# Block products for the streamed second matmul of the first MLP, in a linear-attention and two-MLP kernel

## The chip, the cores and the metric

One core of a Trainium2 chip (trn2). The metric is device time in microseconds, the median of several executions. In the profile PE is TensorE, DVE VectorE, ACT ScalarE; SP is the sync engine, whose queue issues nearly every DMA here.

## The reference

Batch 4, 8 heads, 768 steps, head size 64; 3072 tokens of 512 features go through two MLPs of width 2048.

```python
state = gamma * state + k_t v_t^T ;  y_t = q_t state / 8      # linear attention, per head
x = y laid out as (3072 tokens, 512)
h = x @ w_in ;  g = h * sigmoid(1.702 h) ;  x = g @ w_out     # first MLP,  512 -> 2048 -> 512
h = x @ w_in2 ; g = max(h,0) + alpha * min(h,0) ; out = g @ w_out2   # second MLP, same shape
```

The weights arrive as float64 words, so the kernel converts them to float32 itself. Every float32 product is made of float32r matmuls over a high and a low part: hi·hi, lo·hi and hi·lo.

## The kernel before

Activations are kept transposed, in blocks of 512 tokens. A matmul is 128x128 by 128x512.

**Stages.** Attention runs in 24 chunks of 128 steps. Token blocks 0 and 1 of the first MLP are computed from resident weights while these are converted (`mlp_h`, `mlp_y`); then comes the streamed part. It works on five pairs of two token blocks each, `PAIRS`: pairs 0 and 1 are blocks 2 to 5 of the first MLP, pairs 2 to 4 are the six blocks of the second.

**Units.** In the streamed part `x @ w_in` is done as seven block products instead of eight (Strassen's scheme in Winograd's form). For one pair and one slice pair of the width (2 x 128 features, eight of them: the code calls it a quad) there are seven units; each is six matmuls on one loaded weight tile `hw` (`h_unit`, line 617). The weight sums that the scheme needs are made once (`conv_sums`, `conv_split`) and stored to DRAM in `wc`; the input sums are made by `x_prep` just before a pair begins. The outputs of the units are added on DVE (line 632) and copied on ACT (line 629) out of two PSUM banks of each of two pools. There are 280 units in 40 groups of seven; below, group 0 is the first, and groups 0 to 15 belong to pairs 0 and 1. The attention chunks 16 to 23 still run among groups 0 to 4.

**Chunks.** `g @ w_out` follows 32 units later (`YLAG`) in chunks of six matmuls, one after each unit. For pairs 2 to 4 it is done in seven block products too: `strassen_y`, line 711, weights `yw`, over two halves of four slice pairs, with sums of g made by `y_split` on DVE (line 660), splits into high and low (`g_split`: ACT line 492, DVE line 493) and sums of the results by `y_out` on DVE (line 722). For pairs 0 and 1 it is plain: 768 matmuls at line 526, weights `woh` and `wol` from `wo`, which holds the converted `w_out` as it is, in a ring of six (`WSTEPS`, `load_wo`); eight chunks follow seven units.

**Order and queues.** The Tile scheduler fixes at build time the order of instructions on every engine, from the program's order and priorities; each engine then runs its queue in that order. `jobs` is a table of slots (two slots for each group of seven units, `base` = 64 being the first) in which conversions (`convert`), stores, sums, loads of x and attention steps are put. SBUF tiles come from a ring of 82 slots of 2 KB per partition (`take`, `give`); raw inputs go through five buffers `ld` of twice that. All loads and stores share SP's queue.

Of the kernel before, what the change touches and what calls it, by code (L numbers as in the profile page):

```python
# [31 lines left out]
WSTEPS = 6  # L32
# [26 lines left out]
IDX_S = 2  # L59
ATT1 = 36  # L60
W2_AT = [7 + m // 2 for m in range(10)] + [16 + m - 10 for m in range(10, 22)] + [32 + 4 * (m - 22) // 5 for m in range(22, 32)]
# [3 lines left out]
def tile_linear_attention_two_mlps(ctx: ExitStack, tc, qk, kv, w1, w2, consts, alpha, out):  # L65
# [34 lines left out]
        for k, l in (("in", 1), ("in", 2), ("out", 2))  # L100
        for i in range(NQ)
    }
    wo = {f: dram.tile([2, P, 512], F32, name=f"wo{f}", tag=f"wo{f}") for f in range(NF)}
# [32 lines left out]
    def issue(limit=RING):  # L136
        while count["issued"] < min(len(order), count["done"] + limit):
            key = order[count["issued"]]
            if key[0] == "x" and ("x", key[1]) not in stored:
                return  # L140
# [73 lines left out]
    def conv_lo(key):  # L214
# [10 lines left out]
        if kind == "in" or layer == 2:  # L225
            raw[key] = t
        else:
            give(t)
# [10 lines left out]
    def store(key):  # L239
        kind, layer, ft = key  # L240
        hi, lo = w_hi[key], w_lo.get(key)
        if kind == "out" and layer == 1:
            put(wo[ft][0], hi)
            put(wo[ft][1], lo)
        else:
            dst, at = wc[kind, layer, ft // 2], W_AT[kind]
            if packed(key) is not None:
                put(dst[at["a22" if kind == "in" else "a11"]], hi)
            elif kind == "out" or ft % 2 == 0:
                first = at["a11" if kind == "in" else "a12"]  # L250
                put_two(dst, first, 0, hi)
                put_two(dst, first, 1, lo)
            else:
                put(dst[at["a22"], :, 0:256], hi[:, 256:])
                put(dst[at["a22"], :, 256:512], lo[:, 256:])
# [6 lines left out]
    def conv_sums(kind, layer, i):  # L262
        a, b = raw.pop((kind, layer, 2 * i)), raw.pop((kind, layer, 2 * i + 1))
# [10 lines left out]
        give(a, b)  # L274
# [120 lines left out]
    def att_x(c):  # L395
# [23 lines left out]
        if c % (2 * BT // C) == 2 * BT // C - 1:  # L419
            stored.add(("x", idx))  # L420
            issue()
# [24 lines left out]

    def x_prep(idx, n):
        which = X_OF[n]
        for k in range(2):
            b11, b12 = halves2(loaded["x", idx, k, 0])  # L450
            b21, b22 = halves2(loaded["x", idx, k, 1])
            sub = lambda o, x, y: nc.vector.tensor_tensor(out=o, in0=x, in1=y, op=ALU.subtract)
            if which == "t2":
                t1, t2 = xt[idx, "t1", k], xt[idx, "t2", k] = take("t1"), take("t2")
                sub(t1, b12, b11)
                sub(t2, b22, t1)
            if which == "t3":
                xt[idx, "t3", k] = take("t3")
                sub(xt[idx, "t3", k], b22, b12)
            if which == "t4":  # L460
                xt[idx, "t4", k] = t = xt.pop((idx, "t2", k))
                sub(t, b21, t)
            if which[0] == "b":
                x_split(idx, n, k, {"b11": b11, "b21": b21, "b22": b22}[which])
# [4 lines left out]
            if which in ("b22", "t4"):  # L469
                done()  # L470
# [105 lines left out]
    def load_y(c):  # L576
        if c < len(ychunks) and ychunks[c][0] == "s":
            _, idx, grp, p, m = ychunks[c]
            load_piece(yw, "yw", "out", PAIRS[idx][0], GQ * grp + m, p)

    ysteps = [(idx, t, f if t == 0 else NF - 1 - f) for idx in range(IDX_S) for t in range(2) for f in range(NF)]
    wkey = [f for _, _, f in ysteps]
    wring = {}
    ychunks = [("o", n, half) for n in range(len(ysteps)) for half in range(2)]
    ychunks += [
        ("s", idx, grp, p, m)
        for idx in range(IDX_S, len(PAIRS))
# [4 lines left out]

    def load_wo(n):
        for f in wkey[n:n + 2 * WSTEPS]:
            if f in wring:
                continue
            if len(wring) == WSTEPS or ("out", 1, f) not in stored:
                return
            wring[f] = take("woh", dtype=F32R), take("wol", dtype=F32R)
            for t, src in zip(wring[f], (0, 1)):  # L600
                nc.sync.dma_start(out=t.bitcast(F32), in_=wo[f][src])
# [45 lines left out]
    def y_split(c):  # L647
        kind = ychunks[c][0]
        with tc.high_priority(HG):
            if kind == "o":  # L650
                _, n, half = ychunks[c]
                if half == 0:
                    idx, t, f = ysteps[n]
# [327 lines left out]
```

## Time and profile before

| | |
|---|---|
| median of 3 runs | 1070.77 us (1069.96 to 1071.54) |
| the profiled execution | 1073.08 us, of which the span is 1071.3 us |
| PE busy | 1052.1 us, 98% of the span |
| DVE busy | 774.2 us, 72% |
| ACT busy | 628.2 us, 59% |
| DMA | 283.5 MB, 265 GB/s in the mean |

Busy time counts an engine's instructions from their start to their end, and these overlap in a full queue, so the distance between two starts is shorter than the mean of one. The DMA share is the mean busy share of the 16 DMA engines.

### The profile page before, as it was taken

Reading aid. Unit: us, or ns where it says so; the run is one execution under the profiler, and the core shown is the slowest. Engines: PE = TensorE matmul, PEld = TensorE weight load, DVE = VectorE, ACT = ScalarE, POOL = GpSimd, SP = SyncE. Lnnn points to the kernel's source line nnn. Section 1 sums busy time; section 2 is a strip of 40 time slices with the busy share of each in tenths; the row PEclk is TensorE's granted clock in tenths of the full one; section 3 lists DMA queues with packets and bytes.
Section 4 is the critical chain, followed back from the end, with each engine's and each line's share of the span. In section 5 each row is a group of like instructions: output and inputs, shape, how many; then the busy total and the mean of one; then the engine's idle time right before and its main releaser. Section 6 shows DMA issues by size and latency. Waiting matters only on the chain.

```text
span 1071.3 us, 16434 instructions
## 1 busy us (share of the span) xinstructions
PE 1052.1 (98%) x5644; PEld 861.1 (80%) x5644; DVE 774.2 (72%) x1370; ACT 628.2 (59%) x1220; POOL 0.2 (0%) x4
## 2 busy tenths in 40 slices
PE   8999999999979999999999999999999999999998
PEld 5788877788758888888888888888888888888887
DVE  6999835455469786556577889699677698677693
ACT  6787724344466475455475766585555675546750
POOL 0000000000000000000000000000000000000000
PEclk9999999999999999999999999999999999999999
DMA  7688659988989997988969998866776566776561
GB/s 288 218 277 314 204 173 343 372 301 290 318 284 314 374 356 253 390 300 275 392 216 325 316 323 292 278 199 228 231 256 186 177 218 201 221 238 198 174 207 70
DMA packets 163156, 283.53 MB, mean 265 GB/s; under 512 B 15744, under 2 KB 63232, under 8 KB 163072
## 3 DMA queue, kind: packets, MB, share of 16 engines
q1 hardware_dynamic: 162784, 282.27, 78.4%
q8 instruction: 45, 0.74, 0.3%
q14 instruction: 39, 0.32, 0.1%
q10 hardware_dynamic: 288, 0.20, 0.1%
HBM read 212.15 MB, written 70.25 MB: 264 GB/s over the span
## 4 chain that ended last, share of the span: by engine, by line
PE 88%; DMA 7%; ACT 2%; DVE 2%; SPq 0%; issue 0%; DVEq 0%; ACTq 0%
PE py L526 24%; PE py L711 21%; PE pa L617 18%; PE pd L617 14%; PE ph L505 7%; DMA ld<-kv 3%; DMA hw<-wcin 1%; PE sc L317 1%; ACT v L310 1%; DMA xsd<-x 1%; PE px L353 1%; DMA ld<-w 1%; PE pu L353 1%; DMA early<-qk 1%; PE px L365 0%; DMA wcin<-slo 0%
## 5 line engine op out<-in xcount | busy, mean ns | idle before, releaser
L617 PE MATMUL pa<-xo,hw 128*128 128x512 f32 x960 | 244.6, 392 | 7.5 <-ACT gw L629 5.6
L617 PEld LDWEIGHTS pa<-xo,hw 128*128 128x128 f32 x960 | 180.4, 189 | 46.7 <-ACT gw L629 6.1
L493 DVE TENSOR_TENSOR gl<-gw,gh 128x512 fp32r<-128x512 f32 x208 | 140.0, 685 | 63.4 <-ACT gh L492 48.6
L617 PE MATMUL pd<-xo,hw 128*128 128x512 f32 x720 | 184.1, 392 | 0.0
L711 PE MATMUL py<-gh,yw 128*128 128x512 f32 x672 | 179.8, 389 | 0.0
L492 ACT CAST gh<-gw 128x512 fp32r<-128x512 f32 x208 | 126.6, 620 | 73.0 <-PE py L711 15.2
L617 PEld LDWEIGHTS pd<-xo,hw 128*128 128x128 f32 x720 | 135.7, 189 | 28.6
L711 PEld LDWEIGHTS py<-gh,yw 128*128 128x128 f32 x672 | 126.2, 188 | 26.1
L711 PE MATMUL py<-gl,yw 128*128 128x512 f32 x336 | 103.6, 389 | 0.0
L526 PE MATMUL py<-gh,woh 128*128 128x512 f32 x256 | 99.6, 389 | 0.0
L526 PE MATMUL py<-gh,wol 128*128 128x512 f32 x256 | 99.6, 389 | 0.0
L483 ACT ACTIVATE t<-gw 128x512 f32<-128x512 f32 x72 | 45.5, 632 | 73.6 <-DVE gw L632 73.0
L485 DVE SCALAR_TENSOR_TENSOR gw<-t,nalpha,gw 128x512 f32<-128x512 f32 x96 | 71.3, 746 | 23.7 <-ACT gw L484 23.1
L526 PE MATMUL py<-gl,woh 128*128 128x512 f32 x256 | 79.3, 389 | 0.0
L711 PEld LDWEIGHTS py<-gl,yw 128*128 128x128 f32 x336 | 63.1, 188 | 13.1
L629 ACT COPY gw<-pa 128x512 f32<-128x512 f32 x80 | 46.6, 583 | 37.0 <-PE pa L617 36.8
L310 ACT ACTIVATE v<-ld,cst 128x64 f32<-128x64 f32 x168 | 43.9, 336 | 40.5 <-DMA ld<-kv 39.8
L632 DVE TENSOR_TENSOR gw<-pd,gw 128x512 f32<-128x512 f32 x80 | 54.7, 685 | 16.2 <-PE pd L617 15.3
L526 PEld LDWEIGHTS py<-gh,wol 128*128 128x128 f32 x256 | 48.1, 188 | 10.0
L526 PEld LDWEIGHTS py<-gh,woh 128*128 128x128 f32 x256 | 48.1, 188 | 10.0
L526 PEld LDWEIGHTS py<-gl,woh 128*128 128x128 f32 x256 | 48.1, 188 | 9.9
L722 DVE TENSOR_TENSOR yc<-py,yc 128x512 f32<-128x512 f32 x59 | 37.9, 682 | 20.5 <-PE py L711 20.5
(94 smaller groups left out, 1572.1 us busy)
## 6 DMA issues: line engine op xcount, KB each, us to landing
hw<-wcin SPq DMA_DIRECT2D x280, 256.0 KB, 4.5
yw<-wcout SPq DMA_DIRECT2D x168, 256.0 KB, 3.1
ld<-w SPq DMA_DIRECT2D x64, 512.0 KB, 5.1
woh<-wo SPq DMA_DIRECT2D x46, 256.0 KB, 5.4
wol<-wo SPq DMA_DIRECT2D x46, 256.0 KB, 5.5
ld<-qk SPq DMA_DIRECT2D x21, 512.0 KB, 5.3
ld<-kv SPq DMA_DIRECT2D x21, 512.0 KB, 5.2
ld<-xsd SPq DMA_DIRECT2D x20, 512.0 KB, 6.0
```

The lines of the kernel that those rows point to most:

```text
L310: nc.scalar.activation(out=v[:, h, :], in_=vt[:, h * D:(h + 1) * D], func=AF.Copy, scale=decay_v[:, h:h + 1])
L483: nc.scalar.activation(out=t, in_=src, func=AF.Relu, scale=-1.0)
L485: nc.vector.scalar_tensor_tensor(out=g, in0=t, scalar=nalpha[:, ft:ft + 1], in1=g, op0=ALU.mult, op1=ALU.add)
L492: nc.scalar.copy(out=gh, in_=g)
L493: nc.vector.tensor_tensor(out=gl, in0=g, in1=gh.bitcast(F32), op=ALU.subtract)
L505: nc.tensor.matmul(out=ph, lhsT=w[:, k * P:(k + 1) * P], rhs=x[:, k, :], start=(n == 0), stop=(n == len(prods) - 1),)
L526: nc.tensor.matmul(out=py[e], lhsT=w, rhs=g, start=(begin and seen[e] == 1), stop=(end and seen[e] == 3))
L617: nc.tensor.matmul(out=ps, lhsT=w[:, 256 * part_ + k * P:256 * part_ + (k + 1) * P], rhs=x[2 * k + low], start=(n in (0, 1, 3) and m == 0) ...
L629: nc.scalar.copy(out=chain[quad, n], in_=ps)
L632: nc.vector.tensor_tensor(out=g, in0=ps, in1=g, op=ALU.add)
L711: nc.tensor.matmul(out=ps[e], lhsT=w[:, at:at + P], rhs=t, start=(fresh and seen[e] == 1), stop=(m == GQ - 1 and seen[e] == 3), skip_group ...
L722: add_ = lambda o, x: nc.vector.tensor_tensor(out=o, in0=ps, in1=x, op=ALU.add)
```

## The change

Pairs 0 and 1 get their `g @ w_out` as block products too: all 280 chunks are now of one kind, one after each unit. For this the first MLP's `w_out` gets sums and an arranged copy in `wc`, as the other three weights have; its float32 words are stored to `wraw` and loaded again later for the sums. The tiles `woh` and `wol`, `wo` and `load_wo` go. The loads of x take eight slot tiles `xl` instead of four `ld` buffers, and are put two slots later for pairs 1 to 4. The second MLP's weight conversions (`W2_AT`), the stores of the first's weights (`STORE_W`) and the sums of `w_in` and `w_out` (`SUMS_IN`, `SUMS_OUT`) get other slots.

```diff
+YLOAD = 28
+SUMS_IN = 37
+SUMS_OUT = [58, 60, 62, 65, 72, 74, 76, 78]
+STORE_W = (28, 1.2)
-W2_AT = [7 + m // 2 for m in range(10)] + [16 + m - 10 for m in range(10, 22)] + [32 + 4 * (m - 22) // 5 for m in range(22, 32)]
+W2_AT = [1 + 2 * m for m in range(5)] + [10 + 1.07 * (m - 5) for m in range(5, 32)]
...
-            give(t)
+            put(wraw[ft // 2][:, ft % 2, :], t)
+            give_stored(t)
...
-        a, b = raw.pop((kind, layer, 2 * i)), raw.pop((kind, layer, 2 * i + 1))
+        if ("raw", i) in loaded and (kind, layer) == ("out", 1):
+            a, b = halves2(loaded.pop(("raw", i)))
+        else:
+            a, b = raw.pop((kind, layer, 2 * i)), raw.pop((kind, layer, 2 * i + 1))
...
+    def x_load(idx):
+        assert ("x", idx) in stored
+        for k in range(2):
+            for d in range(2):
+                for t in range(2):
+                    xl[k, d, t] = take("xl")
+                    nc.sync.dma_start(out=xl[k, d, t], in_=xsd[idx][k, :, d, t])
...
     def y_chunk(c):
-        if ychunks[c][0] == "o":
-            _, n, half = ychunks[c]
-            idx, t, f = ysteps[n]
-            first, end = n % NF == 0, n % NF == NF - 1
-            mlp_y(1, 2 * PAIRS[idx][1] + t, f, first, end, None, wring[f], range(2 * half, 2 * half + 2))
...
-    def strassen_y(c):
-        _, idx, grp, p, m = ychunks[c]
+        idx, grp, p, m = ychunks[c]
...
-            s = slot + 3 if key[1] == 2 else ATT1 + 1 + 4 * i if i < 4 else base + 2 * i - 6
+            s = slot + 3 if key[1] == 2 else SUMS_IN + 3 * i if key[0] == "in" else SUMS_OUT[i]
...
-            y_turn(min(8 * past // NU, old) + max(0, past - old * NU // 8))
+            y_turn(past)
```

How instructions stand now is read from the built programs. The first place is DVE's queue about the end of pair 0: from the add of unit 54 (pair 0's last add) to the first add of pair 1, that of unit 57. Before, the first add is row 527 and the second row 541; the last twelve rows are these (`gl` is a low part of g, `xo` an input of pair 1's units, `cvt` a weight in conversion, `slo` a low part of a weight sum).

```order
530 L445 TENSOR_TENSOR xo<-ld,xo 128x512
531 L493 TENSOR_TENSOR gl<-gw,gh 128x512
532 L445 TENSOR_TENSOR xo<-ld,xo 128x512
533 L281 TENSOR_TENSOR slo<-s_4404,shi 128x512
534 L183 TENSOR_SCALAR cvt<-cvt 128x512
535 L186 TENSOR_SCALAR cvt<-cvt 128x512
536 L493 TENSOR_TENSOR gl<-gw,gh 128x512
537 L445 TENSOR_TENSOR xo<-t_4333,xo 128x512
538 L493 TENSOR_TENSOR gl<-gw,gh 128x512
539 L445 TENSOR_TENSOR xo<-t_4343,xo 128x512
540 L189 ISA cvt<-cvt,cvr 128x1024
541 L632 TENSOR_TENSOR gw<-pd,gw 128x512
```

In the changed kernel the two adds are rows 588 and 612 of DVE's queue; the last twelve rows are these (`t` is an input sum of pair 1, `xl` its loaded x).

```order
601 L452 TENSOR_TENSOR xo<-xl,xo 128x512
602 L452 TENSOR_TENSOR xo<-t_4626,xo 128x512
603 L467 TENSOR_TENSOR t_4513<-xl,t_4513 128x512
604 L467 TENSOR_TENSOR t_4523<-xl,t_4523 128x512
605 L511 TENSOR_TENSOR gl<-gw,gh 128x512
606 L274 TENSOR_TENSOR s_4703<-cvt 128x256
607 L274 TENSOR_TENSOR s_4703<-cvt,s_4702 128x256
608 L226 TENSOR_TENSOR wlo<-cvt,whi 128x512
609 L452 TENSOR_TENSOR xo<-t_4513,xo 128x512
610 L452 TENSOR_TENSOR xo<-t_4523,xo 128x512
611 L511 TENSOR_TENSOR gl<-gw,gh 128x512
612 L636 TENSOR_TENSOR gw<-pd,gw 128x512
```

Between the two adds stood 13 instructions, and now 24: row 593, not shown, counts two. The inputs of pair 1 were mostly made earlier, and stand here now.

The second place is SP's queue at the same point. Before, these rows are around the last load of pair 1's x (row 284 has it; `w` is a raw weight, `wcin` and `wcout` are arranged weights and sums on their way to DRAM).

```order
281 L233 DMA wcout_1_105<-wb 128x512
282 L233 DMA wcout_1_105<-whi 128x2x256
283 L233 DMA wcout_1_105<-wlo 128x2x256
284 L146 DMA ld<-xsd_84 128x1024
285 L146 DMA ld<-w 128x1024
286 L565 DMA hw<-wcin_7_95 128x512 x2
287 L601 DMA woh<-wo_126 128x512
288 L601 DMA wol<-wo_126 128x512
```

In the changed kernel these rows are around the loads of the same x, `xl`.

```order
342 L583 DMA hw<-wcin_7_95 128x512
343 L583 DMA yw<-wcout_2_106 128x512
344 L238 DMA wcout_1_113<-wb 128x512
345 L148 DMA ld<-w 128x1024
346 L238 DMA wcout_6_110<-shi 128x2x256
347 L238 DMA wcout_6_110<-slo 128x2x256
348 L238 DMA wcout_6_110<-shi 128x2x256
349 L238 DMA wcout_6_110<-slo 128x2x256
350 L462 DMA xl<-xsd_84 128x512 x8
351 L583 DMA hw<-wcin_7_95 128x512
352 L583 DMA yw<-wcout_3_107 128x512
353 L583 DMA hw<-wcin_0_88 128x512
```

The weight tile of unit 54 is loaded by row 342 and that of unit 55 by row 351, with 15 other transfers between them, eight of them the loads of x in one piece; before, the x was loaded in four pieces far apart.

## Rows read from the trace of the kernel before

**Rows 1.** The page, part 1: busy us, share of the span, instructions of each engine.
```profile
span 1071.3 us, 16434 instructions
PE 1052.1 (98%) x5644; PEld 861.1 (80%) x5644; DVE 774.2 (72%) x1370; ACT 628.2 (59%) x1220; POOL 0.2 (0%) x4
```
**Rows 2.** Windows: stretch, length, PE, PEld, DVE, ACT, POOL busy, clock, DMA share, GB/s.
```profile
150.00:180.00 30.00, 29.48 (x267) 22.94 (x264) 15.89 (x33) 12.16 (x32) 0.00 (x0) 1.00 0.99 341
180.00:210.00 30.00, 30.00 (x303) 23.69 (x301) 14.93 (x31) 12.32 (x39) 0.00 (x0) 1.00 1.04 369
245.00:330.00 85.00, 76.50 (x671) 60.82 (x671) 48.64 (x99) 46.69 (x121) 0.00 (x0) 0.96 0.87 291
330.00:360.00 30.00, 30.00 (x134) 24.84 (x133) 27.84 (x57) 19.38 (x35) 0.00 (x0) 1.00 1.05 372
360.00:390.00 30.00, 30.00 (x134) 24.86 (x133) 23.11 (x43) 16.71 (x31) 0.00 (x0) 1.00 1.04 366
330.00:690.00 360.00, 359.96 (x1588) 297.86 (x1587) 262.05 (x470) 214.69 (x385) 0.00 (x0) 1.00 0.91 319
690.00:1067.00 377.00, 377.00 (x1664) 312.26 (x1664) 287.40 (x455) 221.69 (x391) 0.00 (x0) 1.00 0.65 201
```
**Rows 3.** The chain that ended last, in order of time: start us, us, what.
```profile
345.15 2.72 PE py L526 x12
651.47 2.72 PE py L526 x12
1022.75 44.89 PE py L711 x198
```
**Rows 4.** Timeline of PE: start us, us, instructions, [idle before and its releaser].
```profile
313.01 1.52 PE L617 MATMUL pd<-xo,hw 128*128 128x512 f32 x6
320.17 2.93 PE L617 MATMUL pa<-xo,hw 128*128 128x512 f32 x6 [5.64 <-ACT gw L629]
322.90 2.72 PE L617 MATMUL pd<-xo,hw 128*128 128x512 f32 x6
```
**Rows 5.** Timeline of ACT, the same stretch.
```profile
316.81 0.66 ACT L176 ACTIVATE cvt<-ld 128x512 f32<-128x512 f32 x1 [3.50 <-DMA ld<-w]
319.56 0.56 ACT L629 COPY gw<-pa 128x512 f32<-128x512 f32 x1
```
**Rows 6.** Timeline of DVE, pieces of two stretches, the rows of each in order.
```profile
383.70 0.68 DVE L445 TENSOR_TENSOR xo<-ld,xo 128x512 fp32r<-128x512 f32 x1
384.30 0.42 DVE L269 TENSOR_TENSOR s<-cvt 128x256 f32<-128x256 f32 x1
384.63 0.68 DVE L452 TENSOR_TENSOR t<-ld,t 128x512 f32<-128x512 f32 x1
385.24 0.68 DVE L445 TENSOR_TENSOR xo<-ld,xo 128x512 fp32r<-128x512 f32 x1
...
868.53 0.74 DVE L485 SCALAR_TENSOR_TENSOR gw<-t,nalpha,gw 128x512 f32<-128x512 f32 x1
869.19 0.68 DVE L452 TENSOR_TENSOR t<-ld 128x512 f32<-128x512 f32 x1
```
**Rows 7.** Waits of DVE from 860 to 905 us: in total us, times, longest.
```profile
DVE gl L493 <- ACT gh L492: 2.2, 2, 1.5
```
**Rows 8.** Groups by line: busy us, mean ns of one, idle before, releasers.
```profile
L526 PE MATMUL py<-gh,woh 128*128 128x512 f32 x256 | 99.6, 389 | 0.0
L492 ACT CAST gh<-gw 128x512 fp32r<-128x512 f32 x208 | 126.6, 620 | 73.0 <-PE py L711 15.2 <-DVE gl L493 12.8 <-PE pd L617 9.0
L660 DVE TENSOR_TENSOR gw<-gw 128x512 f32<-128x512 f32 x48 | 31.5, 683 | 0.2
L722 DVE TENSOR_TENSOR yc<-py,yc 128x512 f32<-128x512 f32 x59 | 37.9, 682 | 20.5 <-PE py L711 20.5
```
**Rows 9.** DMA issues: tiles, queue, count, KB each, median us to landing.
```profile
hw<-wcin SPq DMA_DIRECT2D x280, 256.0 KB, 4.5
yw<-wcout SPq DMA_DIRECT2D x168, 256.0 KB, 3.1
ld<-xsd SPq DMA_DIRECT2D x20, 512.0 KB, 6.0
```

More of the change, by code (lines that the diff above doesn't have):

```diff
@@ L31 @@
 LAG = 1
-WSTEPS = 6
 WARM = 12
@@ L99, in tile_linear_attention_two_mlps @@
         (k, l, i): dram.tile([NU, P, 512], F32, name=f"wc{k}{l}_{i}", tag=f"wc{k}{l}_{i}")
-        for k, l in (("in", 1), ("in", 2), ("out", 2))
+        for k in ("in", "out") for l in (1, 2)
         for i in range(NQ)
     }
-    wo = {f: dram.tile([2, P, 512], F32, name=f"wo{f}", tag=f"wo{f}") for f in range(NF)}
+    wraw = [dram.tile([P, 2, 512], F32, name=f"wraw{i}", tag=f"wraw{i}") for i in range(NQ)]
     stored = set()
@@ L138, in issue @@
             key = order[count["issued"]]
-            if key[0] == "x" and ("x", key[1]) not in stored:
+            if key[0] == "raw" and key not in stored:
                 return
@@ L227, in conv_lo @@
         else:
-            give(t)
+            put(wraw[ft // 2][:, ft % 2, :], t)
+            give_stored(t)
+            if ft % 2:
+                stored.add(("raw", ft // 2))
         if layer == 2:
@@ L241, in store @@
         hi, lo = w_hi[key], w_lo.get(key)
-        if kind == "out" and layer == 1:
-            put(wo[ft][0], hi)
-            put(wo[ft][1], lo)
-        else:
[L246 to L255, printed above, removed]
+        dst, at = wc[kind, layer, ft // 2], W_AT[kind]
+        if packed(key) is not None:
+            put(dst[at["a22" if kind == "in" else "a11"]], hi)
+        elif (kind == "in") == (ft % 2 == 0):
+            first = at["a11" if kind == "in" else "a12"]
+            put_two(dst, first, 0, hi)
+            put_two(dst, first, 1, lo)
+        else:
+            name, m = ("a22", 1) if kind == "in" else ("a11", 0)
+            put(dst[at[name], :, 0:256], halves(hi)[m])
+            put(dst[at[name], :, 256:512], halves(lo)[m])
         stored.add(key)
@@ L273, in conv_sums @@
         add_(s4, a12, s2, ALU.subtract)
-        give(a, b)
+        if (kind, layer) == ("out", 1):
+            done()
+        else:
+            give(a, b)
         sums[kind, layer, i] = (s12, s34)
@@ L576, in load_y @@
     def load_y(c):
-        if c < len(ychunks) and ychunks[c][0] == "s":
-            _, idx, grp, p, m = ychunks[c]
+        if c < len(ychunks):
+            idx, grp, p, m = ychunks[c]
             load_piece(yw, "yw", "out", PAIRS[idx][0], GQ * grp + m, p)
[L581 to L587, printed above, removed]
+    ychunks = [
+        (idx, grp, p, m)
+        for idx in range(len(PAIRS))
         for grp in range(NQ // GQ)
@@ L591, in tile_linear_attention_two_mlps @@
     ]
[L593 to L601, printed above, removed]
     chain = {}
@@ L785, in convert @@
         job(slot + 2, conv_lo, key)
-        if key[2] % 2 and (key[0] == "in" or key[1] == 2):
+        if key[2] % 2:
             i = key[2] // 2
-            s = slot + 3 if key[1] == 2 else ATT1 + 1 + 4 * i if i < 4 else base + 2 * i - 6
-            job(s, conv_sums, key[0], key[1], i)
+            s = slot + 3 if key[1] == 2 else SUMS_IN + 3 * i if key[0] == "in" else SUMS_OUT[i]
+            job(s, conv_sums, key[0], key[1], i, load=(("raw", i),) if key[:2] == ("out", 1) else ())
             job(s + 1, conv_split, key[0], key[1], i)
@@ L813, in tile_linear_attention_two_mlps @@
     for idx in range(len(PAIRS)):
[L814 to L817 removed]
+        job(base + 16 * idx - (12 if idx == 0 else 3), x_load, idx)
     for n in range(NU):
[L819 removed]
+        job(base - 11 + 1.5 * n, x_prep, 0, n)
     def src_of(key):
@@ L911, in y_turn @@
             turn["chunk"] += 1
-    old = 4 * NF * IDX_S
     for u in range(len(units)):
+        if u == YLOAD:
+            for c in range(YRING):
+                load_y(c)
         h_unit(u)
```

53 lines of the change are left out of this document (17 added, 36 removed).

## The prediction

> **What bounds the kernel now.** I read the engines' busy times first [rows 1]: PE is busy for 98% of the span, DVE for 72%, ACT for 59%. Shares over the whole span don't tell which engine limits which stage, so the windows come next [rows 2]. From 330 to 690 us, where pairs 0 and 1 are in their second half, PE is busy for 359.96 of 360 us, and from 690 to the end for 377.00 of 377. DVE has 262 and 287 us of work there and waits for PE. Only the stretch from 245 to 330 us, attention beside the first units, loses time: 8.5 of 85 us.
>
> A busy PE is not yet the price of a matmul, since matmuls overlap. The group at line 526 shows 389 ns for one [rows 8], but the chain of waits shows twelve in 2.72 us and 198 in 44.89 us [rows 3], which is 0.227 us for each. That is what a matmul costs on the path, in the old form (line 526) and in block products (line 711) alike, so from 330 us on a removed matmul is worth 0.227 us as long as everything else keeps up.
>
> Second, who is next. DVE's durations overlap too: in its timeline 512-column instructions start 0.60 us apart when its queue is full, 256-column ones 0.33 and those with a scalar operand 0.66 [rows 6]. DMA runs at 319 GB/s between 330 and 690 us, and at 366 and 372 in its first 60 us, with the 16 engines busy all the time (share 1.04 and 1.05) [rows 2]. So three resources are near their limit in the stage that the change touches.
>
> **The change part by part.**
>
> *Matmuls.* Eight products become seven: 768 matmuls go and 672 come. 96 x 0.227 = **21.8 us** less on PE. The number of chunks behind the last unit stays 32, so the end of the program is as before.
>
> *DVE.* Counted in the two orders, DVE gets 192 more instructions: 48 low parts of g (each block product splits its own sum), 64 sums of g, 40 more adds of results with 8 copies fewer, 16 low parts and 32 quarter-tile sums for `w_out`. 160 x 0.60 + 32 x 0.33 = 107 us. Nearly all of it lands in groups 5 to 21 of seven units. There the changed order has 423 instructions at 0.60, 141 at 0.33 and 21 at 0.66: 314 us, where before had 300, 135 and 22: 239 us. PE's part of these groups falls to 1420 matmuls, 322 us. So on average DVE is just below PE (98%), and the question is how unevenly it lies. I summed it group by group, by the adds of line 632 as marks. Two stretches stand over PE:
> - groups 8 to 10: 93 x 0.60 + 28 x 0.33 = 65.0 us of DVE beside 252 matmuls, 57.1 us: 7.9 over. At its entry stand the inputs of pair 1 in one piece, the first place shown above: 24 instructions between two adds where 13 stood.
> - groups 16 to 19: 117 x 0.60 + 32 x 0.33 + 13 x 0.66 = 89.4 us beside 354 matmuls, 80.3 us: 9.1 over. The inputs of pair 2 and the sums of pair 1 meet the second MLP's gates and the last conversions.
>
> Before, the same groups had 36 and 59 us of DVE, far below PE. Who waits when DVE is late is its add of a unit's output: PE's unit two later writes the same bank again. A chunk, a unit and a chunk lie between, 18 matmuls or 4.1 us, of which the add itself takes 0.7. So each stretch can hide 3.4 us, and 17.0 over become 17.0 - 6.8 = 10.2 us of waiting.
>
> DVE also waits for ACT's high parts in a packed stretch: 2.2 us in the 45 from 860 to 905 us [rows 7], 5%. On 154.4 us that is 7.6; part of it falls where DVE has slack, and I take half, 3.8. Sum for DVE: **14.0 us** given back. Its bounds: nothing, if the slack is larger than the add shows (before, DVE ran without a pause around 384 and 869 us [rows 6] and PE lost nothing in these windows), and 17.0 + 7.6 = 24.6 us with no slack at all.
>
> *ACT.* 72 more instructions, at most 0.62 us each [rows 8]: 45 us. Between 330 and 690 us it was busy for 215 of 360 us [rows 2]; the idle time hides them, and I cost them at nothing. If it were not idle where they stand, they would come in as the waits of DVE for ACT, priced above.
>
> *Transfers.* `w_out` is stored arranged, with sums, and its float32 words go out and come back; `yw` is 280 loads where 168 and 92 were. That is some 20 MB more. Counted in the order, groups 5 to 21 carry 426 transfers and 119.3 MB, before 110.7 MB. Over PE's 322 us this needs 371 GB/s; groups 6 to 8 alone need 25.2 MB in 57.1 us, 441 GB/s. The best full windows showed 369 and 372 [rows 2]. I cost it at nothing, since what is slow in groups 6 to 8 gives DVE the time that it lacks there, and stores can wait; the other end is the second rival.
>
> *Loads of x in slots, two slots later.* At the second place shown, 15 transfers, 4.2 MB, stand between the weight tiles of units 54 and 55. At 370 GB/s they take 11 us, and a landing takes 4.5 us more [rows 9]; six units of prefetch are 16 us. That is just enough, so nothing, at the other end some 4 us at each of the pairs 1 and 2. Behind the late x are ACT and DVE, which make the inputs in order.
>
> *Stage before 330 us.* PE waits 5.64 us for ACT at 320 us and then runs twelve matmuls at half pace, 2.93 and 2.72 us for six [rows 4]: 8.2 us in all. ACT stood behind a raw weight that was still on its way [rows 5]. Conversions of the second MLP now begin six slots earlier, among the attention chunks, and share the five buffers with them; x no longer does. The stall can go (-8.2) or come twice (+8.2); I take 0, as nothing in the order favours one.
>
> **Sum.** The profiled execution took 1073.1 us, 2.3 over the median. 1073.1 - 21.8 + 14.0 = 1065.3, and 2.3 less is **1063.0 us** for the median.
>
> **The rivals.**
>
> *DVE hides it all.* PE stays the bound everywhere. For it: DVE's total in groups 5 to 21 is below PE's, and PE rode through packed DVE stretches before. Against: two stretches over PE by 8 and 9 us. Time: 1070.8 - 21.8 = 1049.0 us.
>
> *Nothing is left.* The work goes from PE to DVE and no slack softens it: 17.0 + 3.8 = 20.8 us back, 1069.8 us, within 0.2% of before, which is about what a measurement here can tell from no change. For it: any transfer that lands late empties DVE's queue, and DVE has no time to catch up.
>
> *Transfers become the bound*, the rival on the other side. The place is groups 5 to 21, the price 119.3 MB over the rate less 321.9 us. It decides at 119.3 / (321.9 + 21.8) = 347 GB/s: below that the kernel gets slower. At the 341 of the window from 150 to 180 us [rows 2], where the share was 0.99, the groups take 350 us, 28 more than PE, and the time is 1077 us; at the mean 319 it would be 1101. For it: over units 34 to 102 many loads of weights for PE now stand only three to six transfers ahead of their use, behind stores in the same queue, so nothing evens out a bad stretch. Against: 366 to 372 GB/s for 60 us on end with PE full.
>
> The Trainium skill (DMA: Bandwidth & Descriptors, section Specifications) gives about 358 GB/s as the share of HBM that one core has; by that figure, an estimate, the groups would take 333 us and the time would be about 1060 us from this cause alone. The windows at 366 to 372 GB/s lie a little above it, so the trace agrees only roughly.
>
> **How the numbers follow.** My forecast, that some two thirds are given back, gets 0.43 with its own range 1053 to 1068.5; everything hidden 0.13; nothing left 0.15; transfers the bound 0.29. So faster by over 0.2% is 0.56, within 0.2% 0.15, slower 0.29. The range takes the hidden case as its low end, 1048, and reaches past the transfers at 341 GB/s, and a second stall of 8.2 us on top of no gain, to 1081.
>
> **What the profile would show.** If I am right: PE's matmuls 96 fewer at the same 0.227 us; PE full up to about group 7, then idle time that the waits put on line 636 (DVE's add) or line 511 around 400 to 450 us and 560 to 620 us, some 14 us in all; DVE over 27 of 30 us in these windows; from group 23 on nothing changed. If all is hidden, PE is full there. If transfers bind, PE's waits name `hw` and `yw`, the DMA share is over 1 for longer than 60 us on end, and DVE waits for `xl` or for PE. I would be wrong above all if the stage before 330 us moved by more than 8 us, or if the in-order queues hold each other up, so that three resources at 94 to 98% cannot be used at once.

## The result: slower, and where the time went

The changed kernel takes 1084.35 us (1083.1 to 1085.5), the kernel before 1070.37 beside it: a ratio of 1.0133, interval 1.0112 to 1.0153. The forecast was 1063.0 us, so the sign is wrong too. The profiled execution took 1084.8 us.

The page of the changed kernel, part 1, answers to [rows 1].

```profile
span 1082.7 us, 16786 instructions
PE 1041.0 (96%) x5548; PEld 845.0 (78%) x5548; DVE 875.2 (81%) x1562; ACT 667.0 (62%) x1292; POOL 0.2 (0%) x4
```

PE has its 96 matmuls less, DVE 101 us more (107 were counted). Two executions below, the profiled one with result stores on GpSimd's queue and one with the sums spread, ran at a lower granted clock throughout (0.75 and 0.56) and are left out, the first with its trace. The windows show where PE is no longer full (columns as in [rows 2]).

```profile
330.00:360.00 30.00, 30.00 (x135) 24.82 (x133) 26.75 (x53) 20.44 (x37) 0.00 (x0) 1.00 1.06 389
360.00:390.00 30.00, 25.32 (x107) 20.26 (x106) 23.41 (x44) 20.69 (x37) 0.00 (x0) 0.97 1.04 386
390.00:420.00 30.00, 26.29 (x103) 20.58 (x102) 29.27 (x54) 21.37 (x40) 0.00 (x0) 0.91 0.93 323
420.00:450.00 30.00, 26.16 (x113) 20.68 (x112) 29.24 (x55) 18.75 (x35) 0.00 (x0) 1.00 0.86 297
450.00:480.00 30.00, 28.82 (x120) 23.43 (x120) 27.00 (x54) 18.63 (x35) 0.00 (x0) 0.94 0.84 313
480.00:510.00 30.00, 24.91 (x100) 19.88 (x101) 22.95 (x41) 12.19 (x22) 0.00 (x0) 0.94 0.93 311
...
570.00:600.00 30.00, 26.83 (x112) 21.66 (x111) 30.00 (x53) 23.61 (x44) 0.00 (x0) 0.94 0.80 265
...
330.00:690.00 360.00, 334.57 (x1415) 270.29 (x1414) 320.59 (x583) 234.51 (x422) 0.00 (x0) 0.97 0.93 329
690.00:1078.00 388.00, 388.00 (x1714) 321.22 (x1713) 297.43 (x472) 228.81 (x405) 0.00 (x0) 1.00 0.68 213
```

The reader is to see two kinds of holes. From 390 to 450 and from 570 us DVE is full and the DMA engines are not. From 360 to 390 us the DMA engines are full (386 GB/s) and DVE is not. Over the stage the transfers ran at 329 GB/s; the prediction had worked out that the changed kernel needs some 370.

A measure that I use below: the distance between the first matmuls of two groups of seven units, minus 0.227 us for each 512-column matmul between them (and 0.055 for an attention matmul). Summed, it tells how much PE lost. It is read from the profiled execution alone, which lies up to 4.6 us from the median (the last table has both), so differences of a few us between kernels are taken from the medians.

| | before | after |
|---|---|---|
| first unit begins | 245.5 us | 247.6 us |
| lost in groups 0 to 4 | 12.8 | 4.4 |
| lost from group 5 on | 0.2 | 39.7 |

2.1 - 8.4 + 39.5 - 21.8 (the matmuls) = 11.4 us, which is the difference of the two spans. So the question is the 39.7 us. PE is idle for 25.4 of 360 us in the window above; the other 14 or so, by subtraction, are slow matmuls, behind idle times. In the timeline of PE (columns as in [rows 4]):

```profile
446.50 0.61 PE L694 MATMUL py<-gl,yw 128*128 128x512 f32 x2
450.47 2.90 PE L621 MATMUL pd<-xo,hw 128*128 128x512 f32 x6 [3.35 <-DVE slo L289]
...
454.63 1.54 PE L621 MATMUL pa<-xo,hw 128*128 128x512 f32 x6
```

Six matmuls take 2.90 us after the wait and 1.54 two steps later; the granted clock from 450 to 480 us is 0.94, so part of it ran at the lower of the two levels (1.2 of 2.4 GHz).

The waits of PE from 330 to 690 us (in total us, times, longest) name everything: transfers 7.6, ACT's copies and high parts 11.8, DVE's low parts 5.3.

```profile
PE pa L621 <- ACT gw L633: 4.9, 2, 3.2
PE pd L621 <- ACT gw L633: 4.9, 3, 4.2
PE pd L621 <- DMA hw<-wcin: 3.8, 2, 3.0
PE pd L621 <- DVE slo L289: 3.4, 1, 3.4
PE pa L621 <- DMA hw<-wcin: 2.0, 1, 2.0
PE py L694 <- ACT gh L510: 2.0, 1, 2.0
PE py L694 <- DVE gl L511: 1.9, 1, 1.9
PE py L694 <- DMA yw<-wcout: 1.8, 2, 1.6
...
```

This list is not the answer, since ACT and DVE themselves wait for raw weights and x. The chain that ended last, from 360 to 392 us, shows that: for 28 us it goes from one transfer to the next, among them raw weights (`ld`) and x (`xl`), before ACT and DVE come in.

```profile
360.65 5.01 DMA hw<-wcin
365.72 6.87 DMA ld<-w
372.61 5.93 DMA ld<-w
378.56 5.52 DMA xl<-xsd
384.11 0.06 issue
384.17 4.86 DMA yw<-wcout
389.04 1.13 ACT xo L451 x2
390.19 0.68 DVE xo L452
390.87 0.60 DVE gw L636
```

### The profile page after: what moved, and what is told of

Its sections match the earlier page's. It is cut to its first block, busy times and chain, and to the rows that moved or that the text cites. A ratio compares the mean times of both kernels' runs of the same rounds, so it can differ in the third digit from the quotient of the medians.

```text
span 1082.7 us, 16786 instructions
## 1 busy us (share of the span) xinstructions
PE 1041.0 (96%) x5548; PEld 845.0 (78%) x5548; DVE 875.2 (81%) x1562; ACT 667.0 (62%) x1292; POOL 0.2 (0%) x4
## 4 chain that ended last, share of the span: by engine, by line
PE 72%; DMA 15%; DVE 8%; ACT 2%; issue 2%; SPq 1%; DVEq 0%; ACTq 0%
PE py L694 27%; PE pa L621 15%; PE pd L621 11%; PE py L544 7%; PE ph L523 7%; DMA yw<-wcout 4%; DMA ld<-w 3%; DMA hw<-wcin 3%; DMA wcout<-shi 2%; DMA ld<-kv 1%; PE sc L325 1%; DVE gl L511 1%; DMA xl<-xsd 1%; PE px L361 1%; DVE a L335 1%
## 5 line engine op out<-in xcount | busy, mean ns | idle before, releaser
L694 PE MATMUL py<-gh,yw 128*128 128x512 f32 x1120 | 303.9, 393 | 3.9 <-ACT gh L510 2.0
L694 PEld LDWEIGHTS py<-gh,yw 128*128 128x128 f32 x1120 | 212.4, 190 | 50.5 <-ACT gh L510 2.6
L621 PE MATMUL pd<-xo,hw 128*128 128x512 f32 x720 | 188.1, 397 | 15.4 <-DMA hw<-wcin 6.3
L694 PE MATMUL py<-gl,yw 128*128 128x512 f32 x560 | 173.9, 392 | 1.9 <-DVE gl L511 1.9
L694 PEld LDWEIGHTS py<-gl,yw 128*128 128x128 f32 x560 | 105.8, 189 | 24.9 <-DVE gl L511 2.8
L657 DVE TENSOR_TENSOR gw<-gw 128x512 f32<-128x512 f32 x80 | 53.3, 684 | 0.9 <-ACT gw L498 0.8
L288 ACT CAST shi<-s 128x512 fp32r<-128x512 f32 x64 | 38.4, 616 | 24.7 <-DVE s L274 9.2
L544 PE MATMUL py<-gh,whi 128*128 128x512 f32 x128 | 51.3, 401 | 0.7 <-ACT gh L510 0.7
L523 PE MATMUL ph<-xhi,whi 128*128 128x512 f32 x128 | 51.4, 401 | 0.4 <-ACT xhi L415 0.4
L178 ACT ACTIVATE cvt<-ld 128x512 f32<-128x512 f32 x64 | 43.0, 673 | 13.8 <-DMA ld<-w 9.5
L498 ACT ACTIVATE gw<-gw 128x512 f32<-128x512 f32 x48 | 30.2, 630 | 34.3 <-DVE gw L636 33.9
```

The costliest lines, as they stand in the source:

```text
L523: nc.tensor.matmul(out=ph, lhsT=w[:, k * P:(k + 1) * P], rhs=x[:, k, :], start=(n == 0), stop=(n == len(prods) - 1),)
L544: nc.tensor.matmul(out=py[e], lhsT=w, rhs=g, start=(begin and seen[e] == 1), stop=(end and seen[e] == 3))
L621: nc.tensor.matmul(out=ps, lhsT=w[:, 256 * part_ + k * P:256 * part_ + (k + 1) * P], rhs=x[2 * k + low], start=(n in (0, 1, 3) and m == 0) ...
L694: nc.tensor.matmul(out=ps[e], lhsT=w[:, at:at + P], rhs=t, start=(fresh and seen[e] == 1), stop=(m == GQ - 1 and seen[e] == 3), skip_group ...
```

## The experiments

Two theories stood first. D: DVE's excess over PE costs the 39.7 us, as forecast, only more. T: the transfers cost them, which the prediction had at nothing.

### Taking one of the two away

**Without sums of g** (`y_split`, pairs 0 and 1 use g itself):

```diff
-            if which == "t2":
+            if which == "t2" and idx < 2:
+                ysplit[c] = g_split(g_of[b22], True)
+                return
+            if which == "t2":
...
-            if which == "t3":
+            if which == "t3" and idx > 1:
```

> Leaves out of the changed kernel the 64 sums and differences of g for pairs 0 and 1 (64 x 0.60 = 38 us of DVE); the block products take g itself, so the output is another one. Transfers and everything else stay. Theory D (DVE is the resource that costs the 39.6 us that PE loses in groups 5 to 20): most comes back, 1050 to 1060 us. Theory T (transfers cost it): nearly nothing comes back, 1080 to 1085 us. Both in turn, each at its own places (by the chain: DVE in groups 8 and 16, 17; transfers in groups 7, 10, 12): about 15 us back, 1070 us.

Measured: 1080.79 us, ratio 1.0103 (1.0069 to 1.0137); 39.1 us are still lost from group 5 on, in a profiled execution 4.1 us over the median. 38 us of DVE work less give 3 or 4 back: D falls as the cause of the whole.

**Without the second MLP's stores** (`store`, `conv_split`; pairs 2 to 4 load from `wc[kind, 1, i]`):

```diff
-        if packed(key) is not None:
+        if layer == 2:
+            pass
+        elif packed(key) is not None:
...
-            for m, t in enumerate((hi, lo)):
+            for m, t in enumerate((hi, lo) if layer == 1 else ()):
```

> Leaves out of the changed kernel the stores of the second MLP's arranged weights and sums (112 x 256 KB, 29 MB, some 25 MB of it in groups 5 to 21); pairs 2 to 4 load the first MLP's weights instead, so the output is another one. The work of PE, DVE and ACT stays. Groups 5 to 21 then carry about 94 MB, 292 GB/s. Theory T: most of the 39.6 us comes back, 1045 to 1055 us. Theory D: hardly anything, 1080 us. Both in turn: 20 to 25 us back, 1060 to 1065 us.

Measured: 1060.9 us, ratio 0.9913 (0.9882 to 0.9944). 15.4 us are lost; 24.3 went with 27 MB of transfers. The standstills of SP's queue before stores of results (shown further below) went from 32.4 to 10.5 us with them, so this run shows that these stores cost the time, and not whether by their bytes or by their place in the queue. Its window shows more DVE work done in the same 360 us than in the changed kernel, beside 271 GB/s:

```profile
330.00:690.00 360.00, 351.45 (x1521) 286.00 (x1521) 334.21 (x607) 247.78 (x448) 0.00 (x0) 0.99 0.81 271
```

**Both edits together:**

> The changed kernel without the second MLP's stores of arranged weights (as in the run without them) and without the sums of g for pairs 0 and 1; the output is another one. The run without the stores still lost 15.2 us in groups 5 to 20. If that rest is DVE's excess over PE: nearly all of it goes, 1046 to 1050 us. If the rest is something else (the loads of x, the order): 1058 to 1062 us.

Measured: 1056.4 us, ratio 0.9873 (0.9841 to 0.9906), between the two expectations. By the medians the sums of g cost 4.5 us here and 3.6 in the changed kernel, and the intervals do not tell the two apart: that they cost more once the transfers are out of the way is not shown (the profiled executions, 8.1 us lost here against 15.4, lie 2.2 us under and 1.1 over their medians). Of the 8.1, 6.6 lie in group 8, around one wait of PE for a high part of g:

```profile
PE py L699 <- ACT gh L512: 4.4, 1, 4.4
```

ACT's queue there, around the copy that PE waits for (it begins at 397.19):

```profile
393.06 0.67 ACT L178 ACTIVATE cvt<-ld 128x512 f32<-128x512 f32 x1
394.18 0.62 ACT L453 CAST xo<-t 128x512 fp32r<-128x512 f32 x1 [0.44 <-DVE t L469]
394.78 0.60 ACT L500 ACTIVATE gw<-pa 128x512 f32<-128x512 f32 x1
395.27 0.61 ACT L453 CAST xo<-t 128x512 fp32r<-128x512 f32 x1
395.78 0.67 ACT L179 ACTIVATE cvr<-ld 128x512 int32<-128x512 uint32 x1
396.58 0.67 ACT L178 ACTIVATE cvt<-ld 128x512 f32<-128x512 f32 x1
397.19 0.62 ACT L512 CAST gh<-gw 128x512 fp32r<-128x512 f32 x1
```

`xo<-t` are inputs of pair 1, and DVE makes `t` in the packed piece that the prediction showed. From 384 to 400 us DVE was busy for all 16 us and ACT for 14.3, beside 133 GB/s: here ACT's queue, too, is all but full.

### Adding transfers to the kernel before

60 stores of 256 KB from a resident tile, one after every second unit:

```diff
+        if 35 <= u < 155 and u % 2:
+            nc.sync.dma_start(out=more[(u - 35) // 2], in_=cst[:, :512])
```

> The kernel before with 60 more stores of 256 KB, one after every second unit from unit 35 to 153, of a resident tile to DRAM that nobody reads (15.7 MB; groups 5 to 21 carry about 126 MB over 341 us of PE, 371 GB/s, the mean rate of the changed kernel there); the work of PE, DVE and ACT stays as before. Theory T in its simple form (the mean rate of 371 GB/s is too much): PE loses 15 us or more in groups 5 to 20, 1085 us or more. Theory D: nothing, 1070 to 1073 us. If transfers bind only where they come in bursts or behind DVE: under 5 us, 1071 to 1076 us.

Measured: 1077.79 us, ratio 1.0078 (1.005 to 1.0106). A miss: nothing tied these stores to their place, and the scheduler put 12.6 of the 15.7 MB ahead of group 0. The first unit began 4.5 us later, and from group 5 on 0.2 us were lost. The second run held them in program order, as `put` does:

```diff
-            nc.sync.dma_start(out=more[(u - 35) // 2], in_=cst[:, :512])
+            put(more[(u - 35) // 2], cst[:, :512])
```

> The kernel before with the 60 extra stores of 256 KB again, now held in program order, since in the last such run the scheduler had put most of them ahead of group 0. Groups 5 to 21 carry 121 MB in this order (110.6 before) beside 341 us of PE work, 355 GB/s, and the loads of weight tiles stand only 2 to 5 us ahead of their use, as in the changed kernel; the work of DVE stays as before, far below PE. Theory Q in its simple form (short leads alone stall PE): 10 us or more lost in groups 6 to 20, 1082 us or more. Theory R: 355 GB/s is below what the windows showed (366 to 389), so 0 to 5 us, 1070 to 1076 us. If both a short lead and a full DVE are needed: also 0 to 5 us.

Measured: 1087.74 us, ratio 1.0162 (1.0138 to 1.0186); 18.2 us are lost from group 5 on, where the same kernel without the stores lost 0.2. So added transfers bring a loss without more work on any engine. Their rate alone does not explain it: 5.9 us are lost in group 8 (395 to 425 us) and 9.9 in groups 20 and 21 (647 to 693 us), and at both the DMA engines were not full when PE fell idle:

```profile
390.00:420.00 30.00, 26.31 (x108) 20.96 (x107) 19.17 (x33) 18.33 (x33) 0.00 (x0) 0.94 0.66 230
480.00:510.00 30.00, 30.00 (x133) 24.58 (x133) 17.53 (x31) 16.34 (x30) 0.00 (x0) 1.00 0.67 231
510.00:540.00 30.00, 30.00 (x134) 24.86 (x133) 16.70 (x32) 12.33 (x22) 0.00 (x0) 1.00 1.05 386
630.00:660.00 30.00, 25.07 (x111) 20.45 (x109) 26.40 (x47) 17.65 (x32) 0.00 (x0) 0.97 0.63 223
```

In the first, the second and the last, the queue of SP stands before a store of results (line 555) that are not made yet, and everything behind it stands too (waits of SP's queue, 400 to 470, 470 to 540 and 610 to 680 us; in the last the queue stood until 654 us, when ACT had copied the first result, line 548, after the matmuls before it):

```profile
SPq L555 <- ACT y L548: 13.1, 2, 12.2
...
SPq L555 <- ACT y L548: 16.9, 2, 15.9
...
SPq L555 <- ACT wb L210: 14.2, 1, 14.2
```

PE's longest wait for a weight tile, 6.6 us, follows the last of them; beside the first its longer wait, 2.8 us, is for a copy of ACT. The second cost PE nothing, and the kernel before had such stops too, up to 12.2 us long, and lost nothing at them; so it takes the added transfers and the stops together. Counted over groups 5 to 21, 351 GB/s were needed and 333 moved.

### Why the rate of the stage is below that of its windows

The changed kernel has the same kind of wait, for DVE's add of a pair's results (330 to 690 us):

```profile
SPq L743 <- DVE yc L706: 32.4, 15, 8.3
SPq L238 <- DVE slo L289: 11.8, 9, 3.0
SPq L583 <- DVE xo L452: 9.6, 2, 9.0
```

The Trainium skill (DMA: Bandwidth & Descriptors, section Anatomy of one DMA — SWDGE (gpsimd) path, which is about DMAs issued by GpSimd) says that any wait for a semaphore happens on the issuing sequencer before dispatch, and that the DMA engines themselves do not wait; the 32.4 us on SP's queue agree. The other two rows are stores of weight sums whose low part is not made, and loads of weight tiles (line 583) that waited for DVE's line 452, once for 9.0 us; whether more tiles would spare that wait was not tried.

Three theories now. R: the bytes beside PE's time decide. Q: loads stand too short ahead of their use. H: the standstills of the queue decide.

**Stores on GpSimd's queue** (`put`), and **loads first** (`load_piece`, in a kernel of its own):

```diff
-        tc.keep_in_program_order(nc.sync.dma_start(out=dst, in_=src.bitcast(F32)))
+        tc.keep_in_program_order(nc.gpsimd.dma_start(out=dst, in_=src.bitcast(F32)))
...
-        nc.sync.dma_start(out=t.bitcast(F32), in_=wc[kind, layer, i][W_AT[kind][W_OF[n]]])
+        with tc.high_priority(HP):
+            nc.sync.dma_start(out=t.bitcast(F32), in_=wc[kind, layer, i][W_AT[kind][W_OF[n]]])
```

> The changed kernel with the stores of arranged weights, sums and raw words issued from GpSimd's queue instead of SP's. Same bytes, same work of PE, DVE and ACT; the loads of weight tiles no longer stand behind stores. In the built order they stand a mean of 12 to 34 us of PE work ahead of their use in groups 4 to 20, where it was 3 to 7. Theory Q (the transfers cost 24 us because loads stand close ahead of their use, behind stores that wait for ACT and DVE in the same queue): about 20 us back, 1060 to 1066 us. Theory R (the rate itself is too high, 119 MB beside 322 us of PE work): little back, 1078 to 1085 us.

> The changed kernel with the loads of hw and yw given a higher priority in the scheduler, on SP's queue as before. Same bytes and same work; the loads then stand a mean of 10 to 19 us ahead of their use in groups 5 to 20, but with single ones still at 0.5 to 3 us. Theory Q: about 10 to 20 us back, 1063 to 1075 us. Theory R: nothing back, 1080 to 1087 us.

Measured: 1153.94 us, ratio 1.0773 (1.0747 to 1.0799), and 1153.55 us, ratio 1.0767 (1.0743 to 1.079). Both missed every expectation: they lost 70 us or more from group 5 on and moved 287 and 288 GB/s in groups 5 to 21, and in the first the first unit began 24.6 us later. Q falls, as far as these two edits test it: with loads well ahead, other transfers come late instead (in the second, ACT waits 10.7 us for x and 7.4 for raw weights between 330 and 690 us). In the first GpSimd was also busy for 173.4 us where it was 0.2, and what its own pace cost was not separated. The Trainium skill (DMA: Bandwidth & Descriptors, section Issuing engines are not separate DMA queues) says that issuing from several engines only saves the time of issuing; the first run agrees in so far as the rate did not rise, at 287 against the changed kernel's 328 GB/s.

**Result stores alone on GpSimd's queue** (first edit), and **the same stores later on SP's** (second: kept in a list and issued five chunks later, without the raised priority of `y_out`):

```diff
-        nc.sync.dma_start(out=dst, in_=y)
+        nc.gpsimd.dma_start(out=dst, in_=y)
...
-        nc.sync.dma_start(out=dst, in_=y)
-        give(y)
+        results.append([4, dst, y, ("x", 2 + j // 2) if p == 6 and e % 2 else None])
```

> The changed kernel with the stores of the results of pairs (line 743) issued from GpSimd's queue, which has nothing else to do; all other stores stay on SP. Between 330 and 690 us SP's queue stood 32.4 us, 15 times, up to 8.3 us, before such a store for DVE's add of the result (line 706), with the loads behind it. Theory H (these standstills empty the DMA engines, and that is what turns 119 MB into a loss): 12 to 20 us back, 1064 to 1072 us. Theory R (bytes alone): 0 to 3 us, 1081 to 1085 us.

> The changed kernel with the stores of the results put on SP's queue five chunks later and without their raised priority, so that the queue no longer stands up to 8.3 us before them; same bytes, same engine work, no other queue used. Theory H (these standstills turn 119 MB into a loss): 10 to 20 us back, 1064 to 1074 us. Theory R (bytes alone): within 3 us of the changed kernel, 1081 to 1087 us.

Measured: 1087.98 us, ratio 1.0164 (1.0133 to 1.0194), and 1078.37 us, ratio 1.007 (1.0044 to 1.0095). The second edit takes the wait away and gives 6 us back, 31.6 us are still lost. So H is a part, a smaller one than expected. The first came out above both expectations; why stays open.

**Fewer bytes.** The second MLP's conversions in the order in which they are needed and later (`W2_AT` up to 43.8), or the same order begun earlier, `[-16 + 4 * m for m in range(5)] + [3 + 1.5 * (m - 5) for m in range(5, 32)]`:

```diff
-W2_AT = [1 + 2 * m for m in range(5)] + [10 + 1.07 * (m - 5) for m in range(5, 32)]
+W2_AT = [1 + 2 * m for m in range(5)] + [11 + 1.26 * (m - 5) for m in range(5, 32)]
+W2_ORDER = [("in", i) for i in range(5)] + [("out", i) for i in range(4)]
+W2_ORDER += [("in", i) for i in range(5, 8)] + [("out", i) for i in range(4, 8)]
```

> The changed kernel with the second MLP's conversions in the order in which their weights are needed and spread over more slots (the last at 43.8 instead of 37.9), so that 4.2 MB of transfers and some 15 us of DVE work move out of groups 5 to 21 to groups 22 and 23. Leads of loads stay at 3 to 6 us. Theory R: the rate falls from 370 to 357 GB/s, some 10 us back, 1070 to 1075 us. Theory Q: only the DVE part comes back, 5 us, 1079 us.

> The changed kernel with the second MLP's conversions in the order of need, begun 17 slots earlier (the first at slot -16) and spread to slot 43.5: 110.1 MB in groups 5 to 21 instead of 119.0, and some 30 us less of DVE work there. Theory R: 342 GB/s needed; half of the 24 us comes back, and a little of DVE's: 1065 to 1072 us, if the stage before 245 us, where the DMA engines are full from 150 to 210 us, loses nothing; some 5 us more if it does. Theory H: only DVE's part, 1078 us.

Measured: 1080.31 us, ratio 1.0084 (1.0062 to 1.0106), and 1076.33 us, ratio 1.0049 (1.0029 to 1.0068). The second lost 12.6 us from group 5 on instead of 39.7, and 21.3 in groups 0 to 4 instead of 4.4: what left one full stage filled another. The first came out where theory Q had it and 5 us above R, the second between R and H.

**The kernel before with the new `W2_AT`:**

> The kernel before with the new slots of the second MLP's conversions (W2_AT) and nothing else. If the spread alone costs or gains: the stall of about 8 us in group 4 goes, as it did in the changed kernel, 1062 to 1065 us, and nothing is lost later. If the new slots are what packs groups 5 to 20: 1075 us or more. Theories T and D both expect little loss later, as the total of the transfers and DVE work stays as before.

Measured: 1069.71 us, ratio 0.9996 (0.9977 to 1.0015). 4 us of the stall in group 4 go, 0.7 us are lost later: the new slots alone cost nothing.

**x loaded earlier:**

```diff
-        job(base + 16 * idx - (12 if idx == 0 else 3), x_load, idx)
+        job(base + 16 * idx - (12 if idx == 0 else 6), x_load, idx)
```

> The changed kernel with the loads of x for pairs 1 to 4 three slots earlier (slot 16 idx - 6 instead of - 3). Same bytes and work. If the 6 us lost in group 8, where pair 1's inputs stand in one piece on DVE, come from x that lands late: 5 to 9 us back (pairs 1 and 2), 1075 to 1079 us. If they come from the work on DVE itself, or are filled again by the wait for transfers: within 3 us of the changed kernel.

Measured: 1086.03 us, ratio 1.0158 (1.0118 to 1.0198): nothing back, in this kernel.

### A version with fewer bytes

The round trip of `w_out`'s float32 words through `wraw` (8.4 MB) can go, since the tiles can stay in SBUF; the sums must then be taken earlier. The second of the two runs here also has the conversions in the order of need and later, up to slot 43.5.

```diff
-            put(wraw[ft // 2][:, ft % 2, :], t)
-            give_stored(t)
...
+        raw[key] = t
...
-            s = slot + 3 if key[1] == 2 else SUMS_IN + 3 * i if key[0] == "in" else SUMS_OUT[i]
+            s = slot + 3 if key[1] == 2 else SUMS_IN + 3 * i if key[0] == "in" else max(slot + 3, 24 + 3 * i)
```

> The changed kernel without the round trip of w_out's float32 words through DRAM (8.4 MB): the sums are taken from the tiles that are still in SBUF, at slot max(slot + 3, 24 + 3 i) instead of slots 58 to 78. Groups 5 to 21 carry 111.4 MB (346 GB/s beside 322 us of PE work) and 20 us less of DVE work, all of it less in groups 5 to 11. Theory R: as in the kernel with early conversions at 110.1 MB, some 12 to 20 us are still lost there, and nothing before group 5: 1057 to 1065 us. Theory H: 1072 to 1080 us.

> The same without the round trip, and with the second MLP's conversions in the order of need and spread to slot 43.5: 106.4 MB in groups 5 to 21, 330 GB/s beside 322 us. Theory R: 6 to 12 us are still lost there, mostly DVE's: 1050 to 1058 us. Theory H: 1070 to 1078 us.

Measured: 1083.36 us, ratio 1.0125 (1.0103 to 1.0148), and 1073.56 us, ratio 1.003 (1.0012 to 1.0048). 25.7 and 13.0 us are lost from group 5 on, in groups 5 to 15 of the second 0.2; but the first unit began at 258.3 and 256.7 us. The upper ends of theory R were 18 and 16 us lower; this later start is 11 and 9 of them. The next two put the sums clear of the attention chunks (`SUMS_IN` is now a list of the same slots), the second with late results as well:

```diff
-SUMS_OUT = [58, 60, 62, 65, 72, 74, 76, 78]
+SUMS_OUT = [12, 16, 30, 34, 52, 54, 56, 58]
...
-            s = slot + 3 if key[1] == 2 else SUMS_IN + 3 * i if key[0] == "in" else max(slot + 3, 24 + 3 * i)
+            s = slot + 3 if key[1] == 2 else SUMS_IN[i] if key[0] == "in" else max(slot + 3, SUMS_OUT[i])
```

> The kernel without the round trip and with later conversions again, but with the sums of w_out taken at slots 12, 16, 30, 34 and 52 to 58 instead of 24 to 45, clear of the attention chunks: in the last such run the first unit began at 256.7 us instead of 247.6, and the loss of 9 us came between 143 and 227 us, where sums and attention shared DVE; in groups 5 to 15 nothing was lost. Theory R with this explanation: the first unit begins at 248 to 251 us and the rest stays, 1064 to 1069 us. If the sums cost as much wherever they stand: 1072 to 1076 us.

> The same, with the stores of results five chunks later and without raised priority, which gave 6 us back in the changed kernel. With few bytes left to catch up, the standstills of SP's queue should cost less here: 0 to 3 us less than the kernel with the sums spread alone, 1062 to 1069 us. If they cost by themselves, whatever the bytes: 5 to 6 us less.

Measured: 1071.86 us, ratio 1.0016 (0.9999 to 1.0033), and 1067.18 us, ratio 0.9973 (0.9959 to 0.9987). The first unit began at 255.3 and 256.3 us, hardly earlier: the sums cost nearly as much at these slots. The late results are worth 5 us here as well. What was left in the second: 8.6 us in group 16, with the inputs of pair 2. So x again, two slots earlier:

```diff
-        job(base + 16 * idx - (12 if idx == 0 else 3), x_load, idx)
+        job(base + 16 * idx - (12 if idx == 0 else 5), x_load, idx)
```

> The last version (sums spread, late results) with the loads of x for pairs 1 to 4 two slots earlier, at 16 idx - 5, where the kernel before had them. That version lost 8.6 us in group 16, where DVE makes pair 2's inputs in one piece and PE waits 5.8 us once for ACT's copy behind them. If the piece is packed because x lands late: 4 to 8 us less, 1060 to 1063 us. If it is DVE's work itself, as in the changed kernel, where loading x earlier brought nothing: within 2 us of that version, 1065 to 1069 us.

Measured: 1060.14 us, ratio 0.9912 (0.989 to 0.9933), faster than both kernels. The loss in group 16 is gone, 5.5 us are lost from group 5 on, and the windows of the stage show PE full beside DVE or the DMA engines, and in one window beside both:

```profile
390.00:420.00 30.00, 30.00 (x134) 24.86 (x133) 29.75 (x53) 22.36 (x42) 0.00 (x0) 1.00 0.80 270
480.00:510.00 30.00, 30.00 (x134) 24.86 (x133) 26.04 (x45) 16.62 (x30) 0.00 (x0) 1.00 1.05 386
570.00:600.00 30.00, 30.00 (x134) 24.59 (x133) 29.83 (x53) 20.31 (x37) 0.00 (x0) 1.00 0.99 331
330.00:690.00 360.00, 356.08 (x1565) 293.15 (x1565) 331.41 (x593) 246.94 (x448) 0.00 (x0) 1.00 0.96 334
```

The main ones in one table: MB of groups 5 to 21 in the built order, the GB/s that these need beside PE's work there, the GB/s moved (the same MB over the time that the groups took), what PE lost from group 5 on in the profiled execution, the time of that execution, and the median.

| kernel | MB | needed | moved | lost us | profiled us | median us |
|---|---|---|---|---|---|---|
| before | 110.6 | 320 | 320 | 0.2 | 1073.1 | 1070.4 |
| before, 60 stores in order | 121.1 | 351 | 333 | 18.2 | 1085.5 | 1087.7 |
| changed | 119.0 | 369 | 328 | 39.7 | 1084.8 | 1084.4 |
| changed, late results | 119.5 | 370 | 337 | 31.6 | 1078.8 | 1078.4 |
| later conversions | 114.8 | 356 | 325 | 34.7 | 1080.3 | 1080.3 |
| early conversions | 110.1 | 340 | 327 | 12.6 | 1075.1 | 1076.3 |
| no round trip | 111.4 | 345 | 319 | 25.7 | 1085.5 | 1083.4 |
| no round trip, later conversions | 106.4 | 329 | 320 | 13.0 | 1072.1 | 1073.6 |
| no round trip, later, sums spread | 108.0 | 334 | 319 | 20.9 | 1074.2 | 1071.9 |
| the same, late results | 108.3 | 334 | 324 | 15.7 | 1071.8 | 1067.2 |
| the same, x earlier | 109.1 | 338 | 335 | 5.5 | 1059.3 | 1060.1 |
| without the second MLP's stores | 91.8 | 284 | 271 | 15.4 | 1062.0 | 1060.9 |

Where PE loses time, "moved" falls below "needed" whatever the cause, so the two columns alone prove nothing of the transfers, and bytes alone do not order the losses: 284 GB/s needed went with 15.4 us, 338 with 5.5. Nor is 337 a limit of the rate: from 250 to 550 us the changed kernel moved 346 GB/s, and the one with late results 358.

## Why the prediction was wrong

**The step that failed is the transfers, costed at nothing.** The numbers in it were right: 119 MB, some 370 GB/s needed. The wrong part is what they were held against, "the best full windows" at 369 and 372 GB/s [rows 2]. No run moved more than 337 GB/s over groups 5 to 21, though many have windows at 380 and more. One reason is shown: between such windows the one in-order queue stands before a store whose data is not there, and 6 us come back where it does not. What else keeps the mean at 337 stays open, since 300 us at 358 occur. The mean of the stage, 319 in [rows 2], is what the kernel before needed with PE full, and no limit; the rival that took the 341 of another stage had the sign, and the transfers as the cause. Taking the second MLP's weight stores away, 27 MB in these groups, gives 24.3 of the 39.7 us back; adding 10.5 MB to the kernel before costs 18, mostly beside stops of the queue. The reason given for nothing, that stores can wait, fails too: weights wait behind them.

**The rival in which transfers become the bound** had the kernel slower if less than 347 GB/s are moved; the changed kernel moved 328 and was slower. But it held one rate for the whole stage, and the experiments show no such rate. Its 1077 us at 341 GB/s was too low.

**DVE, 14.0 us.** Without the second MLP's stores 15.4 us are lost, near the forecast size and at its places (8.0 us in group 8, 5.1 in groups 16 to 19). That this is DVE's excess is not shown: leaving 38 us of DVE work out gave 4.5 us of it back, and 3 or 4 in the changed kernel, and group 8 still lost 6.6. Nor need a DVE that is all but full cost as much: the last version does 331 us of DVE work in the 360 us and loses 5.5.

**Loads of x, nothing.** In the changed kernel that is what moving them showed. In the last version, with fewer bytes and late results, two slots were worth 7.0 us (1067.18 to 1060.14; 6.5 by the ratios to the kernel before): about the end given as 4 us for each of two pairs, but nearly all of it in group 16, at pair 2. Which of the differences between the two kernels brings it out is not shown.

**Matmuls, 21.8 us.** Right: 5548 against 5644, at the same pace. **Stage before 330 us, 0 within 8.2.** The stall went, as one of the two ends had it: 8.4 us less lost, the first unit 2.1 later. **ACT, nothing.** Not quite: the longest wait of PE without the second MLP's stores, 4.4 us with and without the sums of g, is for a high part in ACT's queue, which was then all but full with pair 1's inputs.

**Trace.** PE was to be full to about group 7 and idle around 400 to 450 and 560 to 620 us: the places came, and with them 360 to 390 and 480 to 510 us, where the transfers are ahead. The sentence on the in-order queues, named as what would make the forecast wrong above all, is what happened, as far as the cause is shown.

## What to carry to other kernels

Hold the bytes that a stage needs against what long stretches have moved, not against the best windows: the windows of 30 us shown or read here went up to 399 GB/s, stretches of 300 us up to 358, and this stage, which needed 369, got at most 337, with loads and stores in one in-order queue. An edit that brings nothing in one version may bring something in the next, so try it again after the bound has moved: loading x three slots earlier gave nothing in the changed kernel, and two slots earlier gave 7 us in a later version. A store whose data comes late belongs later in the queue, behind the loads that others wait for: 6 and 5 us in two kernels. And compare a few microseconds by medians: one profiled execution can lie 4 us beside them.

## What the runs showed of the hardware that was not expected

Windows of 30 us at 380 to 399 GB/s stand in the same stage as others at 230 to 330, in kernels with and without a full DVE; the most over 300 us was 358 GB/s (late results, 250 to 550 us), and 337 over groups 5 to 21. With loads given long leads, PE lost more from group 5 on instead of less: 70 us with the stores on GpSimd's queue and 95 by priority, where it had been 40. Slow matmuls after waits made some 14 of the 39.7 us, over half as much as the idle time itself (25.4).
